# Splitting a global column sum between TensorE and VectorE, with a short fill on ScalarE between the first store and the first reload

## The chip, the cores and the metric

One Trainium2 chip, one of its cores. The metric is the device time of one execution in microseconds (us), median of several runs. Of the 33 runs of the kernel before in the three sessions of the experiments, 28 lie within 0.3% of their session's median. Every run is on record with a state: all timed runs used here are recorded as fast, and single looks as unknown. A difference under 2% is called "same".

## The reference

The input is an image of 384 x 384 pixels with 384 channels, bfloat16, so 113 MB. The kernel size `k` is 1.

```python
def reference(x, w1d):
    g = jnp.einsum("bhwc->bc", x) / (H * W)      # mean of each channel over the image
    s = _sigmoid(g * w1d[0])                     # one gate per channel
    return x * s[:, None, None, :]               # every pixel times its gate
```

The gate depends on the whole input. Done literally, x would be read twice. The kernel guesses the gate from the first 512 pixels, applies the guess while it streams x once, sums all of x on the way, and compares the true gate with the guess at the end, bit for bit in bfloat16. Only if they differ does a second pass run.

## The kernel before

Pixels are laid out as 1152 rows of 128 partitions. The first 12 rows are loaded as one small block (4 of them give the early gate), the rest as 19 tiles of 60 rows, 5.9 MB each, in 4 slots of on-chip memory. Per tile: load, sum on TensorE, multiply by the gate on VectorE in place, store from the same slot; the next load into a slot waits until the slot's store has landed.

```python
FIRST, EARLY, TILE, SLOTS, BOTH = 12, 4, 60, 4, 3
# ... cut ...
        def one(e, s):                                   # TensorE: sum one tile
            e.wait_ge(ready, 1).then_inc(ready, -1)
            add_rows(e, 1, slot(s) * C, TILE, False, False).then_inc(
                plan.sems["tensor"], 1
            )                                            # 45 matmuls of 512 columns
# ... cut ...
    def put(place, n, r0, to=None):                      # VectorE: gate; ScalarE's queue: store
        to = place if to is None else to
        plan.op("vector", gate(to, place, n, s_early), ...)
        plan.final.append(
            plan.dma("scalar", dram(o_rows, r0, n), at(to, n), reads=rows(to, n))
        )
# ... cut ...
    for k in range(n_tiles):
        if k >= SLOTS:
            put(slot(k), TILE, row0(k - SLOTS))
            load(slot(k), TILE, row0(k))                 # SyncE's queue
        there = rows(slot(k), TILE)
        plan.relay(ready, "gpsimd", "tensor", there, there, ["acc1"])
```

Loads go out on SyncE's queue, stores on ScalarE's. `Planner` records every operation and derives the waits. TensorE runs its sums as a loop over 4 tiles, so its program holds 4 x 45 matmuls.

## Time and profile before

| | before |
|---|---|
| median of the runs before the prediction | 529.54 us (529.05 to 530.78) |
| span of the profiled execution | 527.2 us |
| bytes moved | 226.52 MB, mean 430 GB/s |
| busy: TensorE, VectorE, ScalarE | 42%, 46%, 1% |

From the page of the kernel before, the busy lines, the DMA slices (40 equal slices of the span, 9 is 90% or more) and the bytes:

```profile
PE 220.1 (42%) x865; PEld 0.2 (0%) x2; DVE 240.1 (46%) x38; ACT 2.7 (1%) x4; POOL 0.3 (0%) x5
DMA  9999999999999999999999999999999999999997
HBM read 113.25 MB, written 113.25 MB: 430 GB/s over the span
```

The only row that is full is the DMA engines'. The mean already suggests the bound, but a mean can hide a stage that is not full, so look at stretches. The view by windows, kernel before; columns are the stretch, its length, the busy time of each engine with its instructions, the granted TensorE clock, the DMA share and GB/s:

```profile
48.00:56.00 8.00, 8.00 (x38) 0.00 (x0) 6.71 (x2) 0.00 (x0) 0.00 (x0) 1.00 0.95 369
56.00:100.00 44.00, 14.68 (x60) 0.00 (x0) 29.92 (x3) 0.00 (x0) 0.00 (x0) 0.69 1.00 434
100.00:480.00 380.00, 160.56 (x630) 0.00 (x0) 164.87 (x14) 0.00 (x0) 0.00 (x0) 0.71 1.00 434
480.00:524.00 44.00, 12.18 (x48) 0.00 (x0) 23.77 (x12) 0.61 (x1) 0.00 (x0) 0.66 0.98 422
```

From 56 to 480 us the rate is 434 GB/s without a hole. One dip, 48 to 56 us, is where the first store joins the loads. (In the narrow slices of the page GB/s swings between 409 and 447; that is only where large packets fall, since the page books a whole packet in one slice. Short windows are rough for the same reason: spread over their length, the packets of 48 to 56 us give 391 GB/s and not 369, so the dip costs about 0.8 us.) The whole 226.52 MB at 434 GB/s takes 522 us, so 5 us of the span are anything else. "The DMA engines bound it" means only that all 16 are occupied at this rate.

The groups of instructions that touch the argument (line, engine, operation, shapes, count; busy us, mean ns of one; idle time before them and what ended it), and two lines of the part on DMA issues (KB each, us from issue to landing):

```profile
L201 DVE TENSOR_TENSOR arena<-arena,s_early 128x23040 bf16<-128x23040 bf16 (+1 forms) x20 | 233.5, 11679 | 250.4 <-PE acc L237 247.0
L237 PE MATMUL acc<-arena,ones 128*128 128x512 bf16 x863 | 219.6, 421 | 265.5 <-PEq L276 265.5
L408 DVE TENSOR_REDUCE wrong<-total 128x1 f32<-128x384 f32 x1 | 0.6, 553 | 0.0
...
out_dram<-arena ACTq DMA_DIRECT2D x19, 5760.0 KB, 49.4
out_dram<-arena ACTq DMA_DIRECT2D x1, 1152.0 KB, 23.5
```

VectorE sat idle 247 us "for TensorE". The timeline of one steady tile shows what TensorE itself had waited for (start us, length us):

```profile
172.79 12.16 DVE L201 TENSOR_TENSOR arena<-arena,s_early 128x23040 bf16<-128x23040 bf16 x1 [15.09 <-PE acc L237]
180.62 27.57 SPq L109 DMA_DIRECT2D arena<-in_x_dram  x2
184.99 27.71 ACTq L109 DMA_DIRECT2D out_dram<-arena  x2
188.68 11.44 PE L237 MATMUL acc<-arena,ones 128*128 128x512 bf16 x45 [15.93 <-PEq L276]
200.16 12.16 DVE L201 TENSOR_TENSOR arena<-arena,s_early 128x23040 bf16<-128x23040 bf16 x1 [15.21 <-PE acc L237]
```

A load landed at 188.5 us (its completion records), and TensorE began 0.15 us later. TensorE and VectorE work on it for 23.6 us, one after the other; a tile comes every 27.2 us, and the two engines can work on two tiles. At 180.62 us the next load was issued, 8 us before the running one had landed, so work was queued; the DMA share was 1.00 from 56 to 480 us.

### The profile page before, as it was taken

The numbers are of one execution on the slowest core, as the hardware profiler recorded it, in microseconds if no ns is written. First come the engines' busy times: TensorE is split into PE (matmuls) and PEld (weight loads), VectorE is DVE, ScalarE is ACT, GpSimd is POOL, SyncE is SP. The second block draws the span as 40 slices with busy tenths as digits, with TensorE's granted clock in tenths as the row PEclk, the third lists the DMA queues.
The fourth block names the chain that finished last, engine by engine and source line by source line (L and its number), as shares of the span: only waits on it lengthen the run. The fifth ranks groups of instructions, "written<-read, shape, count | busy, mean of one in ns | idle before, by whom it ended". The sixth has DMA issues, their size and how long they took to land. (4 is left out here: it accounts for less than half of the span.)

```text
span 527.2 us, 1066 instructions
## 1 busy us (share of the span) xinstructions
PE 220.1 (42%) x865; PEld 0.2 (0%) x2; DVE 240.1 (46%) x38; ACT 2.7 (1%) x4; POOL 0.3 (0%) x5
## 2 busy tenths in 40 slices
PE   0389471080807161625343343526261708080900
PEld 0000000000000000000000000000000000000000
DVE  0229958008090808171625353443536261708940
ACT  1000000000000000000000000000000000000000
POOL 0000000000000000000000000000000000000000
PEclk9999876586757676676869595858585858585865
DMA  9999999999999999999999999999999999999997
GB/s 392 425 425 414 440 447 427 413 447 444 434 409 447 444 434 409 447 444 434 416 437 447 437 413 437 447 441 409 437 447 444 409 434 447 444 416 427 442 447 331
DMA packets 6196, 226.52 MB, mean 430 GB/s; under 512 B 690, under 2 KB 690, under 8 KB 690
## 3 DMA queue, kind: packets, MB, share of 16 engines
q10 hardware_dynamic: 3314, 122.10, 53.6%
q1 hardware_dynamic: 2880, 104.40, 46.1%
q8 instruction: 1, 0.02, 0.0%
q14 instruction: 1, 0.01, 0.0%
HBM read 113.25 MB, written 113.25 MB: 430 GB/s over the span
## 5 line engine op out<-in xcount | busy, mean ns | idle before, releaser
L201 DVE TENSOR_TENSOR arena<-arena,s_early 128x23040 bf16<-128x23040 bf16 (+1 forms) x20 | 233.5, 11679 | 250.4 <-PE acc L237 247.0
L237 PE MATMUL acc<-arena,ones 128*128 128x512 bf16 x863 | 219.6, 421 | 265.5 <-PEq L276 265.5
L344 DVE TENSOR_SCALAR w_scaled<-w_all 128x1 f32<-128x1 f32 x2 | 0.2, 153 | 14.5 <-PE w_all L335 14.5
L335 PE MATMUL w_all<-w_one,ones 1*128 1x1 bf16 x1 | 0.2, 158 | 15.5 <-DMA w_one<-in_w1d_dram 15.5
L308 DVE TENSOR_TENSOR total<-total,acc 128x128 f32<-128x128 f32 (+2 forms) x11 | 4.5, 408 | 0.3
L392 ACT ACTIVATE arena<-total,w_scaled 128x384 bf16<-128x384 f32 x1 | 0.6, 615 | 485.9 <-DVE total L308 485.9
L329 ACT ACT_TABLE_LOAD x1 | 1.3, 1283 | 2.3 <-issue 2.3
L306 DVE COPY total<-acc 128x384 f32<-128x384 f32 x1 | 0.6, 558 | 1.2 <-PE acc L237 1.2
L400 DVE TENSOR_TENSOR total<-arena,s_early 128x384 f32<-128x384 uint16 x1 | 0.6, 559 | 0.7 <-ACT arena L392 0.7
L366 ACT ACTIVATE s_early<-total,w_scaled 128x384 bf16<-128x384 f32 x1 | 0.6, 615 | 16.0 <-DVE total L308 16.0
L352 DVE MEMSET ones<- 128x128 bf16 x1 | 0.2, 165 | 1.0 <-PEq L514 1.0
L235 PE MATMUL acc<-arena,ones 128*128 128x512 bf16 x1 | 0.6, 610 | 0.0
L408 DVE TENSOR_REDUCE wrong<-total 128x1 f32<-128x384 f32 x1 | 0.6, 553 | 0.0
L329 ACT ACTIVATE warm<-warm 128x1 f32<-128x1 f32 x1 | 0.2, 203 | 0.0
L414 DVE CAST redo<-wrong 128x1 int32<-128x1 f32 x1 | 0.2, 154 | 0.0
L235 PEld LDWEIGHTS acc<-arena,ones 128*128 128x128 bf16 x1 | 0.1, 105 | 0.0
L335 PEld LDWEIGHTS w_all<-w_one,ones 1*128 1x128 bf16 x1 | 0.1, 99 | 15.5 <-issue 15.5
L514 POOL MEMSET const-bfloat16-1.0<- 128x1 bf16 x1 | 0.1, 102 | 0.0
L514 POOL MEMSET const-uint8-127<- 128x1 uint8 x1 | 0.1, 102 | 0.0
L514 POOL MEMSET const-float32-0.0<- 128x1 f32 x1 | 0.1, 99 | 0.2 <-issue 0.2
L514 POOL MEMSET const-float32-1.0<- 128x1 f32 x1 | 0.1, 99 | 0.0
L351 POOL MEMSET warm<- 128x1 f32 x1 | 0.1, 98 | 0.5 <-POOLq L514 0.5
## 6 DMA issues: line engine op xcount, KB each, us to landing
out_dram<-arena ACTq DMA_DIRECT2D x19, 5760.0 KB, 49.4
arena<-in_x_dram SPq DMA_DIRECT2D x16, 5760.0 KB, 35.6
arena<-in_x_dram ACTq DMA_DIRECT2D x3, 2880.0 KB, 27.6
arena<-in_x_dram SPq DMA_DIRECT2D x3, 2880.0 KB, 36.4
arena<-in_x_dram SPq DMA_DIRECT2D x1, 1152.0 KB, 10.3
out_dram<-arena ACTq DMA_DIRECT2D x1, 1152.0 KB, 23.5
w_one<-in_w1d_dram ACTq DMA_DIRECT2D x1, 0.0 KB
```

What stands on the lines that cost most here:

```text
L201: return lambda e: e.tensor_tensor(to_v, v, s_b, ALU.mult)
L235: loaded.append(e.matmul(bank, weights, moving, start=start, stop=stop))
L237: return e.add_instruction(mybir.InstMatmult(name=nc.get_next_instruction_name(), engine=mybir.EngineType.PE, ins=[e.lower_ap(moving), e.l ...
L306: emit = lambda e, part=part, of=of: e.tensor_copy(part, of)
L308: emit = lambda e, part=part, of=of: e.tensor_tensor(part, part, of, ALU.add)
L329: lambda e: e.activation(warm[:, 1:2], warm[:, 0:1], ACT_F.Sigmoid),
L335: lambda e: e.matmul(w_all[:, 0:1], ones[0:1, :], w_one[0:1, 0:1], start=True, stop=True),
L366: lambda e: e.activation(s_early[:], total[:], ACT_F.Sigmoid, scale=w_scaled[:, 0:1]),
L392: lambda e: e.activation(s_true, total[:], ACT_F.Sigmoid, scale=w_scaled[:, 1:2]),
L400: lambda e: e.tensor_tensor(total[:], s_true.bitcast(U16), s_early[:].bitcast(U16), ALU.not_equal),
L408: lambda e: e.reduce_max(wrong[:], total[:], axis=mybir.AxisListType.X),
L514: nc = _bacc.Bacc("TRN2", target_bir_lowering=False, num_devices=1)
```

## The change

The intent: take 8 of a tile's 60 rows from TensorE, which is off its full clock (0.73 on average), and give them to VectorE, which is idle half of the time. VectorE adds 8 rows to 384 sums in float32, and at the end its sums are split in three bfloat16 terms, which three matmuls add over the partitions. Besides, ScalarE fills 8 spare rows after the first store has landed, and the first load into the freed slot waits for that: a pause in the form of work. Stores go out on ScalarE's queue too, so the main loop now issues the stores of tiles 0 and 1 ahead of the pause; otherwise the second, which in the changed kernel went out at 65.7 us, would stand in ScalarE's program behind a pause that began at 74.3 us.

```diff
-FIRST, EARLY, TILE, SLOTS, BOTH = 12, 4, 60, 4, 3
+FIRST, EARLY, TILE, SLOTS, BOTH, OWN, PAUSE = 12, 4, 60, 4, 3, 8, 8
@@ TensorE's sum of a tile
-            add_rows(e, 1, slot(s) * C, TILE, False, False).then_inc(
+            add_rows(e, 1, slot(s) * C, TILE - OWN, False, False).then_inc(
@@ new
+    def sum_own(k):
+        r0 = slot(k) + TILE - OWN
+        view = at(r0, OWN).rearrange("p (t c) -> p c t", t=OWN)
+        to = part if k else own
+        ... reduce_sum(to[:], view, axis=X) on VectorE, then own += part ...
+    def join_own():
+        ... own as three bfloat16 terms, three matmuls, added to total ...
+    def pause(r0):
+        to = at(base + FIRST + 1, PAUSE)
+        plan.op(
+            "scalar",
+            lambda e: e.activation(
+                to, warm[:, 0:1].broadcast_to([P, PAUSE * C]), ACT_F.Sigmoid
+            ),
+            reads=["warm"],
+            writes=rows(r0, 1) + ["pause"],
+        )
@@ main loop
         if k >= SLOTS:
-            put(slot(k), TILE, row0(k - SLOTS))
-            load(slot(k), TILE, row0(k))
+            for i in range(2) if k == SLOTS else () if k < SLOTS + 2 else (k - SLOTS,):
+                sum_own(i)
+                put(slot(i), TILE, row0(i))
+            if k == SLOTS:
+                pause(slot(k))
+            load(slot(k), TILE, row0(k), reads=["pause"] if k == SLOTS else ())
@@ end
     put(slot(last), TILE, row0(last), slot(n_tiles))
+    sum_own(last)
     put(base, FIRST, 0)
+    join_own()
```

More of the change, by code (lines that the diff above doesn't have):

```diff
@@ L182, in bass_standalone__channel_attn_eca__vision_kernel @@
     total = nc.alloc_sbuf_tensor("total", [P, C], F32)
+    own = nc.alloc_sbuf_tensor("own", [P, C], F32)
+    part = nc.alloc_sbuf_tensor("part", [P, C], F32)
+    terms = nc.alloc_sbuf_tensor("terms", [P, 3 * C], BF16)
     n_arena = nc.sbuf_bytes_remaining // (2 * C)
@@ L189, in bass_standalone__channel_attn_eca__vision_kernel @@
     w_all = nc.alloc_psum_tensor("w_all", [P, WIDE], F32)
+    acc_own = nc.alloc_psum_tensor("acc_own", [P, WIDE], F32)
     def at(r0, n):
@@ L204, in bass_standalone__channel_attn_eca__vision_kernel @@
     base = SLOTS * TILE
-    assert (n_rows - FIRST) % TILE == 0 and base + FIRST < n_arena
-    assert FIRST % 4 == EARLY % 4 == TILE % 4 == 0 and EARLY + 4 < FIRST
+    assert (n_rows - FIRST) % TILE == 0 and base + FIRST + 1 + PAUSE <= n_arena
+    assert FIRST % 4 == EARLY % 4 == (TILE - OWN) % 4 == 0 and EARLY + 4 < FIRST
     last = n_tiles - 1
@@ L218, in bass_standalone__channel_attn_eca__vision_kernel, with load @@
     plan = Planner(nc, "a", 70)
-    def load(place, n, r0, queues=("sync",)):
+    def load(place, n, r0, queues=("sync",), reads=()):
         i = 0
@@ L226, in load @@
                 dram(x_rows, r0, n)[:, i * C : (i + m) * C],
+                reads=reads,
                 writes=rows(place + i, m),
@@ L311, in add_banks @@
             plan.op("vector", emit, reads=[f"acc{group}", "total"], writes=["total"])
+    def sum_own(k):
[3 more added lines that the diff above has]
+        plan.op(
+            "vector",
+            lambda e: e.reduce_sum(to[:], view, axis=mybir.AxisListType.X),
+            reads=rows(r0, OWN),
+            writes=["part" if k else "own"],
+        )
+        if k:
+            plan.op(
+                "vector",
+                lambda e: e.tensor_tensor(own[:], own[:], part[:], ALU.add),
+                reads=["own", "part"],
+                writes=["own"],
+            )
+    def join_own():
+        for i in range(3):
+            term = terms[:, i * C : (i + 1) * C]
+            plan.op(
+                "vector",
+                lambda e, term=term: e.tensor_copy(term, own[:]),
+                reads=["own"],
+                writes=[f"term{i}"],
+            )
+            if i < 2:
+                plan.op(
+                    "vector",
+                    lambda e, term=term: e.tensor_tensor(
+                        own[:], own[:], term, ALU.subtract
+                    ),
+                    reads=["own", f"term{i}"],
+                    writes=["own"],
+                )
+        for i in range(3):
+            term = terms[:, i * C : (i + 1) * C]
+            plan.op(
+                "tensor",
+                lambda e, i=i, term=term: mm(
+                    e, acc_own[:, :C], ones[:], term, i == 0, i == 2
+                ),
+                reads=["ones", f"term{i}"],
+                writes=["acc_own"],
+            )
+        plan.op(
+            "vector",
+            lambda e: e.tensor_tensor(total[:], total[:], acc_own[:, :C], ALU.add),
+            reads=["acc_own", "total"],
+            writes=["total"],
+        )
     def put(place, n, r0, to=None):
@@ L322, in put @@
             plan.dma("scalar", dram(o_rows, r0, n), at(to, n), reads=rows(to, n))
+        )
+    def pause(r0):
+        to = at(base + FIRST + 1, PAUSE)
+        plan.op(
+            "scalar",
+            lambda e: e.activation(
+                to, warm[:, 0:1].broadcast_to([P, PAUSE * C]), ACT_F.Sigmoid
+            ),
+            reads=["warm"],
+            writes=rows(r0, 1) + ["pause"],
         )
@@ L382, in bass_standalone__channel_attn_eca__vision_kernel @@
     for k in range(n_tiles - SLOTS, last):
+        sum_own(k)
         put(slot(k), TILE, row0(k))
     put(slot(last), TILE, row0(last), slot(n_tiles))
+    sum_own(last)
     put(base, FIRST, 0)
+    join_own()
     add_banks(1, copy=False)
```

## The prediction

> **What bounds the kernel now.** The DMA engines: the page's slices show them at 9 tenths or more in 39 of 40. They moved 226.52 MB in a 527.2 us span. By the trace's packet records the rate is flat at 433 to 434 GB/s from about 56 to 524 us; 226.52 MB at 434 is 522 us. [...] Only about 5 us are not pure transfer: about 2 until packets flow, near 1 where the first store joins the loads (369 GB/s in the stretch 48 to 56 us), some tenths in the early loads, about 2 at the end, where the last store's 16 completions spread from 525.1 to 527.2 us.
>
> TensorE (42% busy) and VectorE (46%) have slack. In steady state a tile takes 27.2 us (a load and a store of 5.9 MB each); its 45 matmuls take 11.5 us, then its gate 12.16. A load goes out when its slot's store lands (SyncE's queue waits 444.8 us in all), still 8 us before the previous load ends, so the load queue never runs dry; stores queue 20 us ahead.
>
> **What the change does.**
> - TensorE: 39 matmuls for 45 per tile, 11.5 to 10.0 us.
> - VectorE: a reduce of 3072 bf16 elements. The trace has a 384-element reduce at 0.553 us; [...] I estimate 3.3 us, plus an add of 0.56. Per tile 12.2 becomes 16.1 us, far under 27.2. The reduce runs beside TensorE's sum, so gates start 1.5 us sooner. At the start the first store goes out at 46.7 instead of 48.3 us, the third at 78.5 instead of 73.8, behind earlier stores anyway.
> - ScalarE: one activation of 3072 elements, about 2.8 us (estimated from 0.20 us for 1 and 0.615 for 384 elements). The first store lands at about 75 us as before, since loads and store share one full pipe. The first reload goes out at about 78 instead of 75.0 us; stores keep the pipe full meanwhile. A shift of phase, no idle.
> - End: 3.9 us of summing before the last 12-row gate, whose store goes out at about 510 instead of 503.7 us; the big store before it runs until 524. Joining the sums adds some 5 us to a check that ended at 508.3 us. Both hidden.
>
> **On the critical path: about nothing.** No byte is removed; start and end skew are not touched.
>
> **Predicted: 529.3 us, 80% range 528.2 to 530.9. Chances: faster by over 2% 0.01, within 2% 0.98, slower by over 2% 0.01.**
>
> **What would show it.** TensorE busy 220 to about 192 us, VectorE 240 to 318, ScalarE up 2.8. DMA slices unchanged, mean 429 to 431 GB/s, plateau 434. The first reload about 3 us later, each load landing later by about that, yet the last store landing at the same time. The reduce near 3.3 us.
>
> **What would make it wrong.** The strided reduce costing several times 3.3 us (above about 14, VectorE paces the tile); the shifted phase emptying a queue once per tile (slices drop to 8); the pause changing how unevenly the 16 DMA engines finish, by up to 2 us; the gate check failing, so that the second pass runs (near double).

## The result, and the profile after

| | before | after |
|---|---|---|
| median | 529.54 us (529.05 to 530.78, 4 runs) | 528.49 us (528.48 to 528.64, 4 runs) |
| ratio | | 0.9977, 95% interval 0.996 to 0.9995 |
| span profiled | 527.2 us | 527.0 us |

Ratios here and below are the mean time of one kernel's fast runs over that of the other's fast runs of the same rounds, so not quite the ratio of the medians quoted; those of the experiments leave out the profiled run, which the medians and ranges include. There is a small gain of 0.2%, and the new kernel's runs lie much closer together; the experiments look into that too.

The page of the changed kernel, the lines that answer to those above:

```profile
PE 198.5 (38%) x754; PEld 0.2 (0%) x2; DVE 353.9 (67%) x81; ACT 5.5 (1%) x5; POOL 0.3 (0%) x5
DMA  9999999999999999999999999999999999999998
HBM read 113.25 MB, written 113.25 MB: 430 GB/s over the span
...
L244 PE MATMUL acc<-arena,ones 128*128 128x512 bf16 x749 | 196.6, 429 | 288.4 <-PEq L283 288.4
L207 DVE TENSOR_TENSOR arena<-arena,s_early 128x23040 bf16<-128x23040 bf16 (+1 forms) x20 | 233.5, 11677 | 78.0 <-PE acc L244 73.6
L327 DVE TENSOR_REDUCE part<-arena 128x384 f32<-128x3072 bf16 x18 | 96.4, 5355 | 67.3 <-DMA arena<-in_x_dram 67.3
L392 ACT ACTIVATE arena<-warm 128x3072 bf16<-128x3072 f32 x1 | 2.8, 2763 | 54.1 <-DMA out_dram<-arena 54.1
...
out_dram<-arena ACTq DMA_DIRECT2D x1, 1152.0 KB, 16.9
```

VectorE went from 240 to 354 us of work and TensorE from 220 to 199, and the row of the DMA engines did not change. The reduce took 5.36 us, not the 3.3 that were predicted. One line moved as predicted although it looks like a gain: the last small store takes 16.9 us from issue to landing in place of 23.5, because it is issued 6.3 us later, behind the same big store. It landed at 527.2 us before and 526.9 us after.

The windows, changed kernel:

```profile
48.00:56.00 8.00, 7.06 (x33) 0.00 (x0) 7.97 (x3) 0.00 (x0) 0.00 (x0) 1.00 0.96 369
100.00:480.00 380.00, 143.99 (x546) 0.00 (x0) 249.30 (x43) 0.00 (x0) 0.00 (x0) 0.69 1.00 434
```

The same dip and the same 434 GB/s. One tile in the timeline:

```profile
189.85 5.38 DVE L327 TENSOR_REDUCE part<-arena 128x384 f32<-128x3072 bf16 x1 [4.73 <-DMA arena<-in_x_dram]
189.99 10.20 PE L244 MATMUL acc<-arena,ones 128*128 128x512 bf16 x39 [17.05 <-PEq L283]
200.22 12.16 DVE L207 TENSOR_TENSOR arena<-arena,s_early 128x23040 bf16<-128x23040 bf16 x1 [4.39 <-PE acc L244]
205.40 0.33 SPq L109 DMA_DIRECT2D arena<-in_x_dram  x1
212.41 0.34 ACTq L109 DMA_DIRECT2D out_dram<-arena  x1
```

The load landed at 189.8 us, 1.3 us later than before, and the stores around it 2.4 us earlier (205.4 in place of 207.8): that is the shift of phase. Sum and gate now end 22.5 us after the load, in place of 23.8, and the store goes out at 212.41 us, where before it was 212.36. What the split saved, the later load took. Neither mattered: the store then waits behind the running one, which lands at 232.6 us (before: 235.0).

### The profile page after: what moved, and what is told of

The parts are those of the page before. It is cut to its first block, busy times and chain, and to the rows that moved or that the text cites. A ratio compares the mean times of both kernels' runs of the same rounds, so it can differ in the third digit from the quotient of the medians.

```text
span 527.0 us, 1015 instructions
## 1 busy us (share of the span) xinstructions
PE 198.5 (38%) x754; PEld 0.2 (0%) x2; DVE 353.9 (67%) x81; ACT 5.5 (1%) x5; POOL 0.3 (0%) x5
## 5 line engine op out<-in xcount | busy, mean ns | idle before, releaser
L244 PE MATMUL acc<-arena,ones 128*128 128x512 bf16 x749 | 196.6, 429 | 288.4 <-PEq L283 288.4
L327 DVE TENSOR_REDUCE part<-arena 128x384 f32<-128x3072 bf16 x18 | 96.4, 5355 | 67.3 <-DMA arena<-in_x_dram 67.3
L334 DVE TENSOR_TENSOR own<-own,part 128x384 f32<-128x384 f32 x18 | 10.0, 558 | 0.6
L244 PE MATMUL acc_own<-terms,ones 128*128 128x384 bf16 x3 | 1.4, 479 | 10.5 <-DVE terms L345 10.5
L327 DVE TENSOR_REDUCE own<-arena 128x384 f32<-128x3072 bf16 x1 | 5.3, 5305 | 0.0
L392 ACT ACTIVATE arena<-warm 128x3072 bf16<-128x3072 f32 x1 | 2.8, 2763 | 54.1 <-DMA out_dram<-arena 54.1
L352 DVE TENSOR_TENSOR own<-own,terms 128x384 f32<-128x384 f32 x2 | 1.1, 558 | 0.1
L345 DVE CAST terms<-own 128x384 bf16<-128x384 f32 x3 | 1.1, 357 | 0.1
L242 PE MATMUL acc<-arena,ones 128*128 128x512 bf16 x1 | 0.6, 608 | 0.0
## 6 DMA issues: line engine op xcount, KB each, us to landing
out_dram<-arena ACTq DMA_DIRECT2D x1, 1152.0 KB, 16.9
```

The costliest lines, as they stand in the source:

```text
L242: loaded.append(e.matmul(bank, weights, moving, start=start, stop=stop))
L244: return e.add_instruction(mybir.InstMatmult(name=nc.get_next_instruction_name(), engine=mybir.EngineType.PE, ins=[e.lower_ap(moving), e.l ...
L327: lambda e: e.reduce_sum(to[:], view, axis=mybir.AxisListType.X),
L334: lambda e: e.tensor_tensor(own[:], own[:], part[:], ALU.add),
L345: lambda e, term=term: e.tensor_copy(term, own[:]),
L352: lambda e, term=term: e.tensor_tensor(own[:], own[:], term, ALU.subtract),
```

## The experiments

All kernels ran beside the kernel before, in three sessions, each on one chip. Twelve ran; two theories were put against each other first.

- **Main theory:** the 16 DMA engines bound the kernel all the way, and compute is hidden.
- **Rival:** the gate on VectorE, or the sum in front of it, holds up the stores.

For the small gain there were two theories at first: A, the pause keeps the first reload from colliding with the stores; B, the split sums do it. Later ones are named where they come.

Each of the 43 transfers of image data left 16 completion records in the profile of the kernel before, and as many in that of the changed kernel; I read them as one for each of the 16 DMA engines. These are the 16 completions of the last column. How far they lie apart is called the spread below.

| kernel | median us (range, runs) | ratio to before | last small store: first to last of 16 completions |
|---|---|---|---|
| before (these three sessions) | 529.33, 529.17, 529.23 (528.43 to 535.52, 11 each) | 1 | 525.1 to 527.2 (first profile) |
| after_again | 528.44 (528.29 to 528.97, 6) | 0.998 (0.9962 to 0.9999) | 525.2 to 526.9 |
| split_only | 528.76 (528.36 to 529.72, 6) | 0.9982 (0.9964 to 1.0001) | 526.1 to 528.2 |
| pause_only | 529.48 (528.61 to 533.37, 6) | 1.0001 (0.9976 to 1.0027) | 525.1 to 531.6 |
| dma_only | 529.86 (529.29 to 532.84, 6) | 1.0015 (0.9989 to 1.004) | 525.0 to 528.0 |
| short_sums | 528.97 (528.76 to 529.84, 6) | 0.9974 (0.993 to 1.0018) | 525.1 to 527.8 |
| both_sums | 529.99 (528.76 to 531.47, 6) | 0.9996 (0.9949 to 1.0042) | 525.1 to 527.6 |
| pad_code | 529.41 (528.79 to 530.65, 6) | 0.9996 (0.9974 to 1.0019) | 525.3 to 528.4 |
| own16 / near_reduce | 528.59 / 528.75 (1 each) | | |
| own28 | 618.56 (1) | | |
| pause_x4 | 584.51 (583.31 and 585.71) | 1.1036 (1.0995 to 1.1077) | |
| pause_x8 | 539.03 (538.32 and 539.74) | 1.0177 (1.0142 to 1.0213) | |

### dma_only: all transfers, no gate

```diff
     def put(place, n, r0, to=None):
-        plan.op("vector", gate(to, place, n, s_early), ...)
         plan.final.append(
-            plan.dma("scalar", dram(o_rows, r0, n), at(to, n), reads=rows(to, n))
+            plan.dma("scalar", dram(o_rows, r0, n), at(place, n), reads=rows(place, n))
```

> Wrong result on purpose: stores send the tile as it was loaded, no gate; the sums stay. All loads and stores remain. If the DMA engines alone bound the kernel: 527 to 531 us, that is nothing gained although VectorE loses 234 us of work. If the gate on VectorE held up anything: 2% or more faster.

Measured: 529.86 us, ratio 1.0015. The result was wrong. From the page of dma_only:

```profile
PE 223.3 (42%) x865; PEld 0.2 (0%) x2; DVE 6.7 (1%) x18; ACT 2.7 (1%) x4; POOL 0.3 (0%) x5
DMA  9999999999999999999999999999999999999997
```

VectorE's busy time fell from 240 to 6.7 us and nothing was gained. The store no longer waits for the sum either (the first one went out at 24.0 us in place of 48.3). The rival falls: neither the gate on VectorE nor the sum in front of it is in the way at the size it had before.

### own16 and own28: how much room VectorE has

`OWN` is 16 or 28 in place of 8; nothing else is changed.

> VectorE sums 16 of 60 rows, TensorE 44. The reduce of 8 rows took 5.35 us where I had estimated 3.3. If the cost is by element (1.74 ns each): 10.7 us for 6144 elements, VectorE about 23.4 us per tile. If it is a fixed cost per output [...]: about 8.4 us. Either way under the 27.2 us of a tile's transfers: total 528 to 530 us.

> VectorE sums 28 of 60 rows. At the measured 1.70 ns an element the reduce takes 18.4 us and VectorE needs about 31 us per tile, over the 27.2 us of a tile's transfers: now VectorE paces, DMA slices fall below 9, and the total is about 655 us by counting 19 tiles of 31.1 us from the first gate. If VectorE had not been hidden by slack in the way I claim (for instance if only waits on TensorE matter), it would stay near 529.

The group of the reduce and the gate in own16, then in own28:

```profile
L207 DVE TENSOR_TENSOR arena<-arena,s_early 128x23040 bf16<-128x23040 bf16 (+1 forms) x20 | 233.4, 11672 | 8.3 <-PE acc L244 4.4 <-DMA arena<-in_x_dram 4.0
L327 DVE TENSOR_REDUCE part<-arena 128x384 f32<-128x6144 bf16 x18 | 189.4, 10523 | 44.2 <-DMA arena<-in_x_dram 44.2
```

```profile
L327 DVE TENSOR_REDUCE part<-arena 128x384 f32<-128x10752 bf16 x18 | 326.8, 18153 | 0.0
L207 DVE TENSOR_TENSOR arena<-arena,s_early 128x23040 bf16<-128x23040 bf16 (+1 forms) x20 | 233.4, 11672 | 0.1
```

In own16 VectorE needs 10.5 + 0.5 + 12.2 = 23.2 us per tile and still waits 44 us in all for loads; the time is 528.59 us. In own28 it needs 18.2 + 0.5 + 12.2 = 30.8 us, over the 27.2 of the transfers, and never waits (idle 0.0 and 0.1). The time is 618.56 us. So the room is real and ends where the arithmetic says, between 23.2 and 30.8 us. The page of own28 shows the bound change hands:

```profile
PE 146.8 (24%) x460; PEld 0.2 (0%) x2; DVE 594.7 (96%) x81; ACT 5.5 (1%) x5; POOL 0.3 (0%) x5
DMA  9999779998979898989898989898999998971891
```

The expected 655 us was too high by a counting error of mine: there are 19 tiles, so 18 follow the first, not 19; and the first reduce could start at 20.3 us on rows that had landed early. Without one period of 31 us the estimate is 624.

### near_reduce: why the reduce took 5.36 us and not 3.3

```diff
-        view = at(r0, OWN).rearrange("p (t c) -> p c t", t=OWN)
+        view = at(r0, OWN).rearrange("p (c t) -> p c t", t=OWN)
```

> As own16, but each of the 384 outputs sums 16 neighbouring elements in place of 16 elements 768 bytes apart (the mean is wrong on purpose). If the stride makes the reduce slow: 6144 elements [...], about 6.5 us. If it is not the stride: as own16. Total 528 to 530 us.

The kernel that ran was built from the changed kernel with `OWN` 8, not 16, so the figures of the expectation have to be halved: 3072 elements, about 3.3 us if the stride is at fault. The group of near_reduce:

```profile
L327 DVE TENSOR_REDUCE part<-arena 128x384 f32<-128x3072 bf16 x18 | 60.3, 3351 | 69.0 <-DMA arena<-in_x_dram 69.0
```

It took 3.35 us, the predicted size. In the real reduce the 8 elements of an output lie 768 bytes apart. From 8 to 16 rows it grows by 5.17 us for 3072 elements, 1.68 ns each, so the extra cost is by element and not by output. With neighbours it is 3.35 us for 3072 elements against 0.553 for the 384 of the check (a float32 reduce), so an estimated 1.04 ns each. Only two distances were run, 2 and 768 bytes. That the distance costs is shown; the reason is not. My estimate had counted the elements and not looked at the access pattern.

### pause_x8 and pause_x4: a longer pause

```diff
             if k == SLOTS:
-                pause(slot(k))
+                for _ in range(8):          # 4 in pause_x4
+                    pause(slot(k))
```

> The pause eight times over, 22.1 us. First reload and third store both at about 96.5 us, their bytes from about 99; the second store ends at 88: the DMA engines stand idle some 11 us and the total is about 539 to 540 us. If pauses never mattered: 528.5.

Measured 539.03 us. The windows of pause_x8:

```profile
85.00:88.00 3.00, 0.00 (x0) 0.00 (x0) 3.00 (x1) 2.97 (x2) 0.00 (x0) 0.85 0.57 246
88.00:100.00 12.00, 0.00 (x0) 0.00 (x0) 11.96 (x3) 8.70 (x4) 0.00 (x0) 0.50 0.43 184
```

The pipe runs dry between the second store, which ends at 88 us, and the bytes of the third: the DMA share is 0.43 for 12 us. Against 434 GB/s, the packets of 85 to 104 us, spread over time, leave 8.8 us unused (11 were expected). The median grew by 10.5 us against the changed kernel, the profiled run (538.32 us) by 9.8: the first of the last 16 completions came 9.1 us later (534.4 us), and their spread was 2.3 us in place of 1.6. Lost DMA time is not made up, as the main theory says. Against the kernel before, the verdict at 2% is "unclear" (1.0142 to 1.0213), but the interval lies clear of 1.

> The pause four times over, 11.1 us. First reload at about 85.5 us; the store in flight lasts to about 88 us alone, so the pipe is not empty before the reload's bytes come: 528 to 530 us. If the length of the pause counted directly: 8 us more, 537.

Measured 584.51 us: a plain miss, and by far the largest surprise. Half the pause of pause_x8 costs more than five times as much. The pipe did not run dry in the pause; the windows of pause_x4 show that the rate falls later, and keeps falling:

```profile
88.00:144.00 56.00, 12.06 (x42) 0.00 (x0) 32.83 (x7) 0.00 (x0) 0.00 (x0) 0.59 1.00 434
144.00:175.00 31.00, 10.07 (x40) 0.00 (x0) 18.46 (x4) 0.00 (x0) 0.00 (x0) 0.67 1.00 416
175.00:300.00 125.00, 39.62 (x150) 0.00 (x0) 70.65 (x12) 0.00 (x0) 0.00 (x0) 0.66 1.00 414
300.00:500.00 200.00, 74.18 (x267) 0.00 (x0) 114.33 (x20) 0.00 (x0) 0.00 (x0) 0.67 0.93 374
```

The DMA share is still 1.00 at 414 GB/s: the engines are busy but slower. With this pause the first reload and the third store go out within 2 us of each other (85.7 and 83.7 us) and both wait for the second store to end at 88; from then on a load and a store start and end together. The completion records show a few of the 16 engines falling behind: the 16 completions of one transfer spread over 0.7 us at 88 us, 2.4 at 115, 7.4 (load) and 10.7 (store) at 205; from 332 to 553 us over 40 for the stores and 20 to 24 for the loads. A load into a slot waits for all 16 completions of the slot's store (in the kernel before, the load issued at 180.62 us followed the last of them by 0.02 us and the first by 3.3), so the slowest engine holds up the next load.

The packet records show which packets are slow. A tile is 8 packets of 46,080 bytes on each engine, normally 1.70 us each. From 144 to 175 us, 32 of 140 store packets took longer, 2.24 us on average, and none of the load packets (after 175 us some load packets did too). The records do not name the engine, so I ordered packets into 16 chains by end and start, and numbered them within their tiles. Of the stores between two loads in this stretch, those that directly followed the load packet of the same number were slow in 30 of 30 cases; those one number behind in 0 of 83 (one more packet, at another distance, was slow). Before 144 us, at distances 1 and 2, none of 210 was slow. In the kernel before, most distances are 3, in the changed kernel 4. A few distances of 0 in other kernels (at most 24 in a run) were not slow, and I cannot tell whether they are exceptions or mistakes in the chains. So: shown is that in pause_x4, with load and store in equal phase, single engines were slow (2.24 us a packet in place of 1.70); that the same rows in both are the condition is a pattern of one run; why the phase should matter is open.

### after_again, split_only, pause_only: where the 0.2% comes from

after_again is the changed kernel once more. In split_only the pause is taken out; in pause_only `OWN` is 0 and every `sum_own` and `join_own` is taken out:

```diff
@@ split_only
-            if k == SLOTS:
-                pause(slot(k))
-            load(slot(k), TILE, row0(k), reads=["pause"] if k == SLOTS else ())
+            load(slot(k), TILE, row0(k))
@@ pause_only
-FIRST, EARLY, TILE, SLOTS, BOTH, OWN, PAUSE = 12, 4, 60, 4, 3, 8, 8
+FIRST, EARLY, TILE, SLOTS, BOTH, OWN, PAUSE = 12, 4, 60, 4, 3, 0, 8
-                sum_own(i)
...
-    join_own()
```

> The changed kernel once more, to see whether the 0.2% (528.49 against 529.54 us) holds on another occasion. If it is an effect: ratio 0.996 to 0.999 and runs within 0.2 us of each other, while the kernel before spreads over 1 us or more. If it was chance: ratio 0.999 to 1.001.

> The sums are split between VectorE and TensorE, no pause on ScalarE. Main theory (the DMA engines bound everything): 528.3 to 530.0 us, ratio 0.996 to 1.001. Theory A for the 0.2% (the pause keeps the first reload from colliding with the stores): as slow as before, about 529.5, with stretched load packets at 80 to 86 us as before had. Theory B (the sums done earlier are what helps): about 528.5, as the changed kernel. First reload at about 74.5 us.

> All sums on TensorE as before, only the pause (2.76 us) and the two stores issued ahead of it. Main theory: 528.3 to 530.0 us. Theory A: about 528.5 and steady, no stretched packets at the first reload, TensorE busy 220 us as before. Theory B: about 529.5 with a spread of 1 us or more. First reload at about 78 us.

The gain repeats: 528.44 us, ratio 0.998; but its runs lie 0.68 us apart and not within 0.2. By the medians the split alone has most of it (528.76), the pause alone none (529.48, with the widest range of the three). That speaks against theory A but does not exclude it: both intervals hold 0.998, and that of split_only just holds 1. Stretched load packets at 83 to 90 us did come back in split_only, as A said, but cost little (8 packets, 0.1 us per engine). More came later: from 95 to 485 us its profile has 61 stretched load packets, 0.8 us per engine together, where the kernel before has 5 with 0.1. This was the slowest of its six runs (529.72 us); whether the others had them is not known.

The last column of the table says where runs differ. The first of the 16 completions of the last store comes at 525.0 to 525.3 us in all these profiles but split_only's (526.1). The kernel ends with the last one, and that varies from 526.9 to 531.6 us. In the profiled run of pause_only (533.37 us, the slowest of its six) one single engine finished late: its completion came 2.5 us after the first of the 16 at 96 us, 4.7 at 343, 6.5 at the end, where the 15th came after 1.5. Summed over the packets and divided by 16, the time above the normal packet length is the same, 1.73 us before and 1.70 after (2.55 in split_only, whose first completion also comes about 1 us later); what differs between those two is how evenly it falls. When the first store joins the loads, one packet per engine is stretched by 0.35 to 1.71 us in the kernel before and by 0.64 to 1.05 in the changed one.

### short_sums, both_sums, pad_code: does TensorE's program matter?

Every profile with 45 matmuls per tile has an instruction packet of 16,384 bytes near the end that occupies one DMA engine for 0.93 us; with 39 or fewer it is absent. (Packets of 8192 bytes come in all of them; in the profiles of the kernel before and the changed one they took 0.31 to 0.57 us.) The DMA queues on the page of pause_only, where this packet came at 501.6 us and the late engine lost another 1.4 us in that very stretch:

```profile
q10 hardware_dynamic: 3314, 122.10, 53.1%
q1 hardware_dynamic: 2880, 104.40, 45.7%
q8 instruction: 1, 0.02, 0.0%
```

Theory F takes this fetch for the cause, theory V the work on VectorE, theory W the amount of work on TensorE.

```diff
@@ short_sums, from the kernel before (8 rows not summed at all)
-            add_rows(e, 1, slot(s) * C, TILE, False, False).then_inc(
+            add_rows(e, 1, slot(s) * C, TILE - 8, False, False).then_inc(
@@ both_sums, from split_only (8 rows summed twice)
-            add_rows(e, 1, slot(s) * C, TILE - OWN, False, False).then_inc(
+            add_rows(e, 1, slot(s) * C, TILE, False, False).then_inc(
@@ pad_code, from short_sums
+            for _ in range(6):
+                one_column = arena[:, slot(s) * C : slot(s) * C + 1]
+                mm(e, pad[:, 0:1], ones[:], one_column, True, True)
```

> The kernel before, with TensorE summing 52 of 60 rows and nobody the other 8 (the mean is wrong on purpose; the gate still rounds to the same value). No work on VectorE added, no pause. Theory F (the 0.2% comes from instruction fetches: every profile with 45 matmuls per tile has an instruction packet of 16384 bytes at 497 to 502 us that holds one DMA engine 0.93 us; those with 39 have 8192 bytes, 0.31 us, instead): no 16384-byte packet, about 528.6 us, ratio about 0.998, spread under 0.8 us. Theory V (VectorE's sums or the shifted gates do it): about 529.3 us, ratio 1.000, spread over 1 us.

> TensorE sums all 60 rows as before and VectorE sums 8 of them once more (the mean is wrong on purpose). No pause. Theory F: the 16384-byte instruction packet is back, about 529.3 us, ratio 1.000, with a spread over 1 us. Theory V: about 528.6 us, as the split alone.

> As short_sums (52 of 60 rows summed, nobody the other 8), but with 6 matmuls of one column added per tile into a spare bank: TensorE's program is as long as that of the kernel before, its work nearly that of short_sums. Theory F (instruction fetch): the 16384-byte instruction packet is back at about 497 us, median 529.1 to 530, some runs over 530. Theory W (the amount of TensorE work, 45 full matmuls against 39, is what makes single DMA engines lag): as short_sums, median 528.6 to 529.0, no run over 530.

Their sums are wrong; the gate rounds to the same value, so the outputs were correct. Measured: short_sums 528.97 us, no run over 530 (its runs lie 1.1 us apart, where theory F had said under 0.8); both_sums 529.99, three of six over 530; pad_code 529.41, two of six over 530. The 16,384-byte packet was there in both_sums (495.1 us) and pad_code (495.3), and not in short_sums. Over all timed runs at this pace, the kernels whose profile has no such packet (the changed one, split_only, short_sums, own16, near_reduce) gave 24 runs, none over 529.84 us. The others (before, pause_only, dma_only, both_sums, pad_code) had 21 of 61 over that, up to 535.52.

So theory V has nothing for it: by the medians VectorE's sums are neither needed (short_sums) nor enough (both_sums). F is favoured over W by pad_code. Neither is settled: the ranges of short_sums and pad_code overlap, and each ratio's interval holds 1. And the traces speak against the fetch itself. In four of the five profiles that have it, the spread of the stores' completions does not grow across it: it stays at 2.4 us in both_sums, 3.1 in pad_code (530.12 us, one of its two runs over 530) and 3.1 in dma_only, and goes from 3.3 to 2.1 in the kernel before. Only in pause_only did it grow, from 5.1 to 6.5 us, and there the engine was 2.5 us behind by 96 us and lost more while single load packets were stretched between 178 and 398 us. So late runs go with the longer TensorE program, but that its fetch makes them late is not shown. What makes one engine drop behind in some runs stays open.

No experiment points to a version that beats the changed kernel by more than noise: 226.52 MB at 434 GB/s leave only some 5 us, and the pause alone gives nothing.

## Why the prediction was right

- **The bound.** Right, and shown, as far as "all 16 DMA engines are occupied" goes: with the gate gone the time was the same (ratio 1.0015), with more work on VectorE too (own16), and an idle stretch of the DMA engines came back in the total (pause_x8).
- **The total.** 529.3 us predicted, 528.49 measured, inside 528.2 to 530.9, "same".
- **TensorE and ScalarE.** 192 us busy predicted, 198.5 measured: the 39 matmuls took 10.2 us in steady state at a somewhat lower granted clock (0.69 from 100 to 480 us, 0.71 before). The pause took 2.76 us, predicted 2.8. The prediction's 2.8 does not come out of the two durations that it names: a straight line through 0.20 us for 1 element and 0.615 for 384 gives 3.5. So this hit does not bear out its working.
- **The mis-sized term.** The reduce: 3.3 us estimated, from a rate that no run had shown by then; 5.36 measured, because of the stride of 768 bytes (near_reduce: 3.35). VectorE's busy time was therefore 354 us and not 318, its third store went out at 83.5 us and not 78.5, and the check ended at 518.1 us. All of it was off the critical path, so the total did not feel it, and a right total says nothing for this estimate. The prediction had set the limit for this step at about 14 us; own28 at 18.2 us crossed it and paced the kernel.
- **The phase.** First reload at 77.1 us (before 75.0, predicted 78, since the first store landed 0.7 us earlier); the loads then landed 1.3 us later, not 3, and the stores 2.4 us earlier. "A shift of phase, no idle" was right for 2.76 us. As a general statement it was too weak: the prediction allowed the pause up to 2 us through uneven DMA engines, and a pause of 11 us cost 55 us in just that way.
- **The small gain.** The prediction had nothing on the critical path. Measured were 0.2%, repeated, and by the medians most of it with the split alone. Where it shows is the completion of the last DMA engine; its cause is open.

## What to carry to other kernels

Here all DMA engines were full for the whole span (9 tenths or more in 39 of 40 slices), and moving work between compute engines bought nothing clear (0.2% at most), and cost nothing until VectorE needed more than a tile's transfer time (23.2 us of 27.2: 528.59 us in one run; 30.8: 618.56). Find that limit first, and read an idle wait back to the load behind it. A pause or any shift of phase between loads and stores has to be measured over several lengths: here 2.8, 11 and 22 us gave 528.5, 584.5 and 539.0 us. Differences of a few tenths of a per cent can be one DMA engine's lateness (the last store of pause_only's profile: first completion at 525.1 us, last at 531.6), so look at the spread of the 16 completions before explaining them by the change.
